# Smaller token blocks early, and scores and outputs in one stretch, in a retention and bilinear FFN kernel

## The chip, the cores and the metric

The kernel runs on one core of one Trainium2 chip. The metric is the device time of one execution in microseconds (us), the median of several runs. Most executions of one kernel agree within 0.3%.

Engine names: PE is TensorE (matmul), PEld its weight loads, DVE is VectorE, ACT is ScalarE, POOL is GpSimd, SP is SyncE, whose queue (SPq) issues the DMAs.

## The reference, cut to what matters

```python
# q, k, v: [8 batches, 8 heads, 576 positions, 64]; weights 512 x 1536 (twice), 1536 x 512
scores = scale * q @ k.T
ret    = (scores * Dmat) @ v            # Dmat[i, j] = gamma_head ** (i - j) for i >= j, else 0
x      = ret.transpose(0, 2, 1, 3).reshape(4608, 512)
out    = ((x @ w_a) * (x @ w_b)) @ w_out
```

The kernel computes the first part in chunks of 128 tokens (36 chunks) with a running state, and the FFN in blocks of tokens. A block of n tokens needs n/128 finished chunks.

## The kernel before: the parts that matter

The FFN block is a generator. Each `yield` gives the cost of a matmul in units of a 512-column matmul, and says whether attention work may be put in at this place. `todo` holds attention work with its place, counted in those units.

```python
ps_ffn = pool("ps_ffn", 3, PS)      # three PSUM banks for pa, pb, po
ps_att = pool("ps_att", 4, PS)      # four for scores, outputs, transposes
...
def ffn_block(tok0, n, runs):
    for count in runs:
        for F in ...:               # 12 F steps: pa = xT . wa (4 matmuls of n columns)
            ...                     # ACT: ha = copy of pa
        for F in ...:               # pb = xT . wb (4 matmuls)
            ...
            nc.vector.tensor_tensor(hT[:, F, 0:n], has[F][:, 0:n], pb[:, 0:n], op=ALU.mult)
            pop()                   # one pending DVE piece: a mask multiply or a scaling
            yield n / 512, True
    for u in range(n // 128):       # po = hT . wo, 12 matmuls of 512 columns, copied out by ACT or DVE
        ...

def second_stage(g):                # states, then scores; the masks go to the pending list
    for i in g[1:]:
        state(i)
    for i in g:
        scores(i)

def third_stage(g):
    flush()                         # empties the pending list
    for i in g:
        outputs(i)                  # into an attention bank; the scaling goes to the pending list
...
blocks = [512, 256, 384, 384] + [512] * ((NTOK - 1536) // 512)
placed = [((6, 7), 145, 178, 194), ((8,), 166, 197, 207),     # chunks, cast, scores, outputs
          ((9, 10), 186, 224, 254)]                           # later pairs: scores 36 before outputs
...
for tb, n in enumerate(blocks):
    for cost, edge in ffn_block(tok, n, runs):
        at += cost
        while todo and edge and at >= todo[0][0]:
            _, fn, args = todo.pop(0)
            fn(*args)
    flush()                         # end of a block: everything pending is emitted at once
    tok += n
```

From chunk 6 on, q and k of a chunk are transposed by a DMA (`turn`), issued on the same SP queue as the loads of q, k, v and the stores of the result.

## Time and profile before

| | before |
|---|---|
| timed median | 346.02 us (345.85 to 346.22) |
| span of the profiled execution | 877.8 us |
| PE busy in it | 854.0 us (97%) |
| 512-column matmuls, start to start, in its timeline (most of them) | 0.62 us |

The profiled execution ran its matmuls 2.9 times slower than the timed ones. Lines of its page: span; busy time, share and instructions of PE and DVE; the chain that ended last.

```profile
span 877.8 us, 6134 instructions
PE 854.0 (97%) x2390; PEld 309.4 (35%) x2426; DVE 162.0 (18%) x272; ACT 112.6 (13%) x229; POOL 84.3 (10%) x121
...
PE 97%; issue 2%; DMA 1%; SPq 0%; POOL 0%; DVE 0%; ACT 0%
```

Groups of instructions of the same trace, by shape (busy us, mean ns of one, idle before and what ended it):

```profile
L349 PE MATMUL po<-wo_sb,hT 128*128 128x512 bf16 x401 | 246.1, 826 | 6.2 <-issue 6.2
...
L358 ACT COPY osb<-po 128x512 f32<-128x512 f32 x19 | 11.1, 586 | 212.7 <-PE po L349 201.8 <-remote 10.9
```

DMA queue timeline of the same trace (start, time the queue spent, instruction). The first line holds the loads back until the weights are in, the last two are transposes of chunks 6 and 7 (one merged line) and of chunk 10:

```profile
37.03 0.64 SPq L406 DMA_DIRECT2D gate<-wo_sb  x1
...
123.42 2.76 SPq L206 DMA_TRANSPOSE qkT<-qkb  x2
...
137.58 2.36 SPq L206 DMA_TRANSPOSE qkT<-qkb  x1
```

How to read it: PE is busy everywhere, and the little that is not PE is spread thin. But a PE at a third of its speed hides every wait for DMA or DVE that a full-speed PE would meet.

### The profile page before, as it was taken

Reading aid. Unit: us, or ns where it says so; the run is one execution under the profiler, and the core shown is the slowest. Engines: PE = TensorE matmul, PEld = TensorE weight load, DVE = VectorE, ACT = ScalarE, POOL = GpSimd, SP = SyncE. Lnnn points to the kernel's source line nnn. Section 1 sums busy time; section 2 is a strip of 40 time slices with the busy share of each in tenths; the row PEclk is TensorE's granted clock in tenths of the full one; section 3 lists DMA queues with packets and bytes.
Section 4 is the critical chain, followed back from the end, with each engine's and each line's share of the span. In section 5 each row is a group of like instructions: output and inputs, shape, how many; then the busy total and the mean of one; then the engine's idle time right before and its main releaser. Section 6 shows DMA issues by size and latency. Waiting matters only on the chain.

```text
span 877.8 us, 6134 instructions
## 1 busy us (share of the span) xinstructions
PE 854.0 (97%) x2390; PEld 309.4 (35%) x2426; DVE 162.0 (18%) x272; ACT 112.6 (13%) x229; POOL 84.3 (10%) x121
## 2 busy tenths in 40 slices
PE   6999999999999999999999999999999999999998
PEld 3322345344344333333333333432333333232223
DVE  4211122222121111211122112121121112201100
ACT  5111112011011101100111011101110011101110
POOL 6040002201011010002100210011000000000000
DMA  9980049350090041025400650066002300000000
GB/s 181 207 152 0 25 90 187 80 88 1 29 199 0 13 102 18 0 50 108 81 1 1 131 108 1 0 112 129 0 1 60 61 0 1 8 28 12 0 13 36
DMA packets 154333, 50.74 MB, mean 58 GB/s; under 512 B 144960, under 2 KB 149824, under 8 KB 154304
## 3 DMA queue, kind: packets, MB, share of 16 engines
q1 hardware_dynamic: 149552, 45.63, 26.6%
q0 software_dynamic: 4752, 4.72, 3.4%
q8 instruction: 19, 0.31, 0.2%
q14 instruction: 10, 0.08, 0.0%
HBM read 37.75 MB, written 9.44 MB: 54 GB/s over the span
## 4 chain that ended last, share of the span: by engine, by line
PE 97%; issue 2%; DMA 1%; SPq 0%; POOL 0%; DVE 0%; ACT 0%
PE pb L329 29%; PE pa L316 29%; PE po L349 28%; PE o L285 2%; PE kv L235 2%; PE o L277 2%; PE w L372 1%; PE tp L218 1%; DMA kf<-in_k_dram 1%; SPq L104 0%; POOL qkb L195 0%; PE sc_2460 L252 0%; PE sc_2449 L252 0%; PE sc_1402 L252 0%; PE sc_3677 L252 0%
## 5 line engine op out<-in xcount | busy, mean ns | idle before, releaser
L329 PE MATMUL pb<-xT,wb_sb 128*128 128x512 bf16 (+2 forms) x471 | 279.9, 775 | 2.7 <-issue 2.7
L316 PE MATMUL pa<-xT,wa_sb 128*128 128x512 bf16 (+2 forms) x472 | 277.3, 769 | 3.6 <-issue 3.1
L349 PE MATMUL po<-wo_sb,hT 128*128 128x512 bf16 (+1 forms) x425 | 253.2, 810 | 6.2 <-issue 6.2
L334 DVE TENSOR_TENSOR hT<-ha,pb 128x512 bf16<-128x512 bf16 (+2 forms) x120 | 76.2, 635 | 457.4 <-PE pb L329 443.3
L329 PEld LDWEIGHTS <-wb_sb 128*128 128x128 bf16 x480 | 82.8, 172 | 173.7 <-issue 168.0
L316 PEld LDWEIGHTS <-wa_sb 128*128 128x128 bf16 x480 | 80.7, 172 | 157.2 <-issue 151.4
L349 PEld LDWEIGHTS <-hT 128*128 128x128 bf16 x444 | 73.1, 169 | 162.1 <-issue 159.0
L322 ACT CAST ha<-pa 128x512 bf16<-128x512 f32 (+2 forms) x120 | 65.2, 544 | 447.1 <-PE pa L316 440.9
L196 POOL TENSOR_TENSOR vb<-vf,vs 128x512 bf16<-128x512 f32 x36 | 37.6, 1044 | 295.1 <-issue 144.3
L189 POOL CAST qkb<-qf 128x512 bf16<-128x512 f32 x30 | 18.3, 611 | 290.5 <-DMA qf<-in_q_dram 274.6
L360 DVE COPY osb<-po 128x512 f32<-128x512 f32 (+1 forms) x17 | 11.5, 676 | 175.5 <-PE po L349 175.5
L358 ACT COPY osb<-po 128x512 f32<-128x512 f32 (+1 forms) x20 | 11.5, 576 | 219.3 <-PE po L349 208.4
L292 DVE TENSOR_TENSOR xT<-o,qs 128x512 bf16<-128x512 f32 (+1 forms) x37 | 24.8, 674 | 46.8 <-PE o L285 46.8
L285 PE MATMUL o<-sT,vb 128*64 128x128 bf16 x288 | 30.4, 379 | 0.0
L235 PE MATMUL kv<-vb,qkb 128*128 128x128 bf16 (+1 forms) x128 | 25.4, 373 | 1.4 <-issue 0.9
L235 PEld LDWEIGHTS <-qkb 128*128 128x128 bf16 (+1 forms) x128 | 17.6, 161 | 22.2 <-issue 20.9
L285 PEld LDWEIGHTS <-vb 128*64 128x64 bf16 x288 | 22.3, 181 | 2.5 <-issue 2.5
L195 POOL CAST qkb<-kf 128x512 bf16<-128x512 f32 x32 | 19.7, 616 | 13.6 <-DMA kf<-in_k_dram 13.5
L252 PEld LDWEIGHTS <-qkT 64*128 64x128 bf16 x288 | 15.4, 135 | 12.6 <-issue 9.8
L218 PE MATMUL tp<-identity,qkb 128*128 128x128 bf16 x48 | 8.1, 362 | 6.0 <-ACT qkb L191 5.3
L372 PE MATMUL w<-identity 128*128 128x512 bf16 x14 | 9.3, 790 | 0.0
L218 PEld LDWEIGHTS <-qkb 128*128 128x128 bf16 x48 | 5.2, 140 | 11.1 <-ACT qkb L191 5.7
(195 smaller groups left out, 194.7 us busy)
## 6 DMA issues: line engine op xcount, KB each, us to landing
out_dram<-osb SPq DMA_DIRECT2D x35, 256.0 KB, 2.2
qf<-in_q_dram SPq DMA_DIRECT2D x32, 256.0 KB, 3.6
kf<-in_k_dram SPq DMA_DIRECT2D x32, 256.0 KB, 4.2
vf<-in_v_dram SPq DMA_DIRECT2D x32, 256.0 KB, 4.7
wo_sb<-in_moe_w_out_dram POOLq DMA_DIRECT2D x3, 512.0 KB, 17.8
qf<-in_q_dram SPq DMA_DIRECT2D x8, 128.0 KB, 3.6
kf<-in_k_dram SPq DMA_DIRECT2D x8, 128.0 KB, 3.5
vf<-in_v_dram SPq DMA_DIRECT2D x8, 128.0 KB, 3.5
```

The source lines that it names most:

```text
L189: nc.gpsimd.tensor_copy(qb, qf)
L195: nc.gpsimd.tensor_copy(kb, kf)
L196: nc.gpsimd.tensor_tensor(vb.rearrange("p (h d) -> p h d", h=H), vf.rearrange("p (h d) -> p h d", h=H), vs[:, i % PER, :].unsqueeze(2).to_ ...
L218: nc.tensor.transpose(tp[:, p, :], natural_qk[w][:, p * 128:(p + 1) * 128], identity)
L235: nc.tensor.matmul(kv[:, p, :], kb[r, sl], vb[r, sl], start=(m in (0, MID) and p == 0), stop=True, skip_group_check=True)
L285: nc.tensor.matmul(o[64 * hi:64 * hi + 64, p, :], vb[:, e0:e0 + 64], sT[:, hi, p, :], start=(m == 0 and p == 0), stop=True, skip_group_che ...
L292: nc.vector.tensor_tensor(xT[:, c0:c1, i * 128:(i + 1) * 128], o[:, c0:c1], qs[:, c0:c1, s0:s0 + 128], op=ALU.mult)
L316: nc.tensor.matmul(pa[:, 0:n], wa_sb[:, c, fs], xT[:, c, tok0:tok0 + n], start=(c == 0), stop=(c == NC - 1))
L322: nc.scalar.copy(ha[:, 0:n], pa[:, 0:n])
L329: nc.tensor.matmul(pb[:, 0:n], wb_sb[:, c, fs], xT[:, c, tok0:tok0 + n], start=(c == 0), stop=(c == NC - 1))
L334: nc.vector.tensor_tensor(hT[:, F, 0:n], has[F][:, 0:n], pb[:, 0:n], op=ALU.mult)
L349: nc.tensor.matmul(po[:, 0:width], hT[:, F, u * 128:(u + 1) * 128], wo_sb[:, F, cols], start=(F == 0), stop=(F == NF - 1))
```

## The change

The intent: (1) blocks of 256 tokens for chunks 4 to 15, so that the FFN needs chunks two at a time and later; (2) from chunk 14, the scores of a pair and the outputs of the pair before it in one stretch, which saves changes of the PE's tiling mode (scores use row tiles, outputs column tiles, the FFN neither). Since the scores then hold all four attention banks, the outputs go to FFN banks. (3) A reordered start, and more buffers.

```diff
-    blocks = [512, 256, 384, 384] + [512] * ((NTOK - 1536) // 512)
+    blocks = [512] + [256] * 6 + [512] * ((NTOK - 2048) // 512)
...
-        o = ps_att.tile([128, HP, 128], FP32, tag="att", name="o")
+        o = (home or ps_att).tile([128, HP, 128], FP32,
+                                  tag="ab" if home else "att", name="o")
...
+    def both_stages(g, following):
+        flush()
+        for i in following:
+            scores(i)
+        masks, later[:] = later[:], []
+        for i in g:
+            outputs(i, home=ps_ffn)
+            flush()
+        later.extend(masks)
...
-    placed = [((6, 7), 145, 178, 194), ((8,), 166, 197, 207),
-              ((9, 10), 186, 224, 254)]
+    placed = [((6, 7), 145, 176, 200), ((8, 9), 186, 238, 264),
+              ((10, 11), 222, 296, 324), ((12, 13), 280, 352, 384)]
...   # start, in the pass that ends with chunk 2: one mask, three of four weight issues,
...   # the casts of chunk 3, then the other mask; the fourth weight issue comes later
```

More of the change, by code (lines that the diff above doesn't have):

```diff
@@ L72 @@
     stage = pool("stage", 5)
-    nat = pool("nat", 5)
-    qkt_pool = pool("qkt", 6)
+    nat = pool("nat", 7)
+    qkt_pool = pool("qkt", 8)
     st_pool = pool("st", 4)
     h_pool = pool("hT", 2)
-    ha_pool = pool("ha", 6)
+    ha_pool = pool("ha", 7)
     o_pool = pool("osb", 4)
@@ L162, in load_w @@
     def load_w(f0, f1):
-        nc.gpsimd.dma_start(wa_sb[:, :, f0:f1], wa_r[:, :, f0:f1])
-        nc.gpsimd.dma_start(wb_sb[:, :, f0:f1], wb_r[:, :, f0:f1])
+        for w_sb, w_r in ((wa_sb, wa_r), (wb_sb, wb_r)):
+            nc.gpsimd.dma_start(w_sb[:, :, f0:f1], w_r[:, :, f0:f1])
+            yield
     def load_wo(i):
@@ L264, in scores, with outputs @@
         later.append(lambda: masked(1))
-    def outputs(i, halves=False):
+    def outputs(i, halves=False, home=None):
         m = i % PER
@@ L300, in outputs @@
             later.append(lambda: scaled(0, HP))
-    blocks = [512, 256, 384, 384] + [512] * ((NTOK - 1536) // 512)
-    WCOLS = [3, 4, 5]
+    blocks = [512] + [256] * 6 + [512] * ((NTOK - 2048) // 512)
+    WRUNS = [3, 4, 5]
     def ffn_block(tok0, n, runs):
@@ L374, in warm @@
                              start=True, stop=True)
-    W1, W2 = 128 * WCOLS[0], 128 * (WCOLS[0] + WCOLS[1])
+    W1, W2 = 128 * WRUNS[0], 128 * (WRUNS[0] + WRUNS[1])
     idle = {0: (0, 0), 1: (0, 3), 2: (2, 4), 3: (1, 4)}
@@ L387 @@
         scores(i)
-        flush()
+        pop()
         if i == 2:
-            load_w(0, W1)
-            load_w(W1, W2)
-        if i < 3:
-            cast(i + 1, "dve" if i == 2 else "act")
+            list(load_w(0, W1))
+            second = load_w(W1, W2)
+            next(second)
+        if i == 2:
+            cast(3, "dve")
+            flush()
+        else:
+            flush()
+            if i < 3:
+                cast(i + 1, "act")
         state(i)
@@ L400 @@
             flush()
-    load_w(W2, DFF)
+    list(second)
+    list(load_w(W2, DFF))
     for i in (0, 1, 2):
@@ L449, in third_stage, with sums @@
             outputs(i)
+    def both_stages(g, following):
+        flush()
+        for i in following:
[3 more added lines that the diff above has]
+            outputs(i, home=ps_ffn)
+            flush()
+        later.extend(masks)
+    def sums(g):
+        for i in g:
+            state(i)
     def one_by_one(what, i):
@@ L468 @@
                  for at, what in zip(places, "CTSA")]
-    placed = [((6, 7), 145, 178, 194), ((8,), 166, 197, 207),
-              ((9, 10), 186, 224, 254)]
-    limit = 1e9
-    for i in range(NCH - 1, 10, -2):
-        g = (i, i + 1) if i + 1 < NCH else (i,)
-        third = min(starts[i] - 16, limit - 60)
-        limit = third
-        placed.append((g, third - 104, third - (30 if i == 11 else 36), third))
+    placed = [((6, 7), 145, 176, 200), ((8, 9), 186, 238, 264),
+              ((10, 11), 222, 296, 324), ((12, 13), 280, 352, 384)]
     for g, zeroth, second, third in placed:
         todo += [(zeroth, ahead, (g[-1],)), (second - 14, first_stage, (g,)),
-                 (second, second_stage, (g,)), (third, third_stage, (g,))]
+                 (second, second_stage, (g,))]
+        if g != placed[-1][0]:
+            todo.append((third, third_stage, (g,)))
+    merged = []
+    limit = 1e9
+    for i in range(NCH - 2, 13, -2):
+        third = min(starts[i] - 16, limit - 58)
+        limit = third
+        merged.insert(0, ((i, i + 1), third))
+    for (g, third), (following, _) in zip([(placed[-1][0], placed[-1][3])] + merged,
+                                          merged + [((), 0)]):
+        todo.append((third, both_stages, (g, following)))
+    for g, third in merged:
+        todo += [(third - 136, ahead, (g[-1],)),
+                 (third - 28, sums, (g[0:1],)), (third - 14, sums, (g[1:],))]
     todo.sort(key=lambda e: e[0])
@@ L484 @@
     for tb, n in enumerate(blocks):
-        runs = WCOLS if tb == 0 else [1] * NF
+        runs = WRUNS if tb == 0 else [1] * NF
         for cost, edge in ffn_block(tok, n, runs):
```

## The prediction

> **What bounds the kernel now.** The profiled execution is not the timed one: its span is 877.8 us, the timed median 346.02 us. In the trace's timeline 512-column matmuls follow each other every 0.62 us. The Trainium skill ("TensorE: Matmul & The Clock Gate", Back-to-back issue gap) gives N/2.4 + 2.5 ns, 216 ns for N = 512; no profile line shows it, but only it fits the timed runs. So I take DVE, ACT, POOL and DMA from the trace, PE from that formula.
>
> Estimate of the timed run: FFN 663,552 columns and 1,392 matmuls, 280 us; attention of chunks 4 to 35 about 490 steps (pairs counted once) of some 60 ns, 30 us (timeline: pairs start 55 to 80 ns apart in bursts); start-up about 22.5 us (first pa at 29.6 us in the trace); tail 4 us. Sum 336.5. About 9.5 us remain: 64 changes of tiling mode (16 groups, four each) and early waits. PE is the bound (chain of waits: PE 97%); gain can only come from those 9.5 us and the start.
>
> **Early waits.** The DMA queue's timeline holds q/k/v loads until 37.0 us (weights first); the last of chunk 8 is issued at 55.8 us. From the transpose of chunk 6 (123.4 us) to that of chunk 10 (137.6 us, plus 4.0 us landing) it takes 18 us. Timed, that starts near 59 us and ends near 78 to 81; PE wants scores of chunk 10 near 77. Estimated wait 1 to 4 us.
>
> **What the change does.**
> 1. Blocks of 256 move those scores from place 224 to 296 (15 us later), in pairs from the start: the early wait goes, -1 to -4 us.
> 2. Merged stages: scores next to outputs, three mode changes per pair in place of four, and one group fewer: 64 to 49. The skill ("TensorEngine Tiling (Array Packing)", Key Properties) says that a mode switch drains TensorE; the slow trace cannot show the cost. Estimate 0.1 us each: -1.5 us.
> 3. Start: mask 0 before the key cast on DVE, one weight issue (0.77 us on POOL) later: -0.5 us.
> 4. 192 more FFN matmuls: +0.5 us (2.5 ns each), up to +1.5 if weight loads show.
> 5. In 256-token blocks an F step is 0.87 us; DVE needs 0.42 (hT) + 0.69 (mask), so it lags after each pair's scores: +0.5 to 1.5 us.
> 6. Outputs take two of three FFN banks. In five places (16 units before a block) a po accumulation is open; if banks rotate strictly, the next po waits for the eviction of the one just finished (ACT copy 0.586 us plus signalling, about 0.8 us): +0 to +4 us. In pa/pb places the hT multiply (0.69 us) hides under the attention.
> More buffers, earlier casts: off the path.
>
> Sum: about -2 us.
>
> **Predicted 344.0 us**, range 340.0 to 348.0. Chances: faster by over 2% 0.06, within 2% 0.91, slower 0.03.
>
> **What would show it.** Right on 6: in the waits view po waits for ACT osb about five times, under 1 us each. Right on 5: pa waits for DVE hT in the small blocks. A profile again slow on PE hides the worth of 1 and 2.
>
> **What would make it wrong.** A mode change costing 0.2 us or more or a longer early wait (faster, 338 to 340); weight loads exposed in every 256-column matmul, or DVE lag chaining through the banks (slower, 349 and more).

## The result, and the profile after

The kernel after takes 346.54 us (346.25 to 346.68, 4 runs), the kernel before 345.94 us on the same chip (345.74 to 346.22, 4 runs). The ratio is 1.0016, 95% interval 0.9999 to 1.0033: no gain, and if anything 0.6 us lost. (A ratio is the mean time of one kernel's fast runs over that of the other's of the same rounds, so it is not quite the ratio of the medians.) The range held the time, but the forecast gain of 2 us did not come.

This trace ran at full PE speed. Its page:

```profile
span 345.0 us, 6595 instructions
PE 328.9 (95%) x2587; PEld 190.3 (55%) x2618; DVE 163.3 (47%) x297; ACT 115.5 (33%) x252; POOL 84.9 (25%) x121
...
PEclk9999999999999999999999999999999999999999
DMA  9999999999799999749399139933994230020002
```

For a fair comparison the kernel before was run once more (run before_again), and that trace was fast too:

> The kernel before, unchanged, for a trace at full TensorE speed (the one given ran its matmuls 2.9 times slower). Time 346 us. If the account of the prediction holds: a first pa near 21.4 us (0.7 later than after's 20.69), mode changes of 93 to 99 ns as in the trace of after, some 64 of them, and a wait of 1 to 4 us before the scores of chunk 10. Rival: the early wait is not there (under 0.5 us) and the two kernels tie because the change removed nothing but a few mode changes.

It took 346.1 us (one run, state unknown; its span of 344.4 us is that of a fast run). Its page:

```profile
span 344.4 us, 6170 instructions
PE 330.4 (96%) x2426; PEld 171.5 (50%) x2426; DVE 160.8 (47%) x272; ACT 112.3 (33%) x229; POOL 85.0 (25%) x121
...
PEclk9999999999999999999999999999999999999999
DMA  9999999999999994911994099507990950020002
```

The DMA row says that the DMA engines are full for the first third of the span in both kernels.

With two traces at full speed a ledger can be made. For each matmul I take the time to the start of the next one, less N/2.4 + 2.5 ns. That is the spacing that the Trainium skill gives for an isolated matmul ("TensorE: Matmul & The Clock Gate", Back-to-back issue gap; for streams it gives less, see the last section). The traces agree with it: the 12 pb matmuls from 23.27 to 25.86 us in the trace of after are 215.8 ns apart. What is left over is a gap, and gaps that equal a matmul missing from the trace are set aside. (In the small blocks none is missing; there every gap over 30 ns counts.) From the first pa to the end:

| ledger, us | before_again | after | after less before |
|---|---|---|---|
| first pa of the FFN | 21.33 | 20.69 | -0.64 |
| 192 more matmuls at 2.5 ns | | | +0.48 |
| changes of tiling mode (76 and 61 in the traces) | 7.28 | 5.84 | -1.44 |
| waits before scores or between outputs up to chunk 12 | 3.10 | 2.40 | -0.70 |
| gaps inside 256-token blocks, between pa, pb | 0.16 | 3.24 | +3.08 |
| sum | | | +0.8 |

The spans differ by 0.6 us. So the two kernels do not tie because nothing happened: 2.8 us were won and 3.6 us lost. Three of these rows need their lines.

**Mode changes.** Timeline of PE, before_again: outputs at 185.92 us, and scores by themselves at 192.57 us:

```profile
184.96 1.03 PE L329 MATMUL pb<-xT,wb_sb 128*128 128x512 bf16 x4
185.92 0.41 PE L277 MATMUL o<-qkT,state 128*64 128x128 bf16 x8
...
192.57 0.62 PE L252 MATMUL sc<-qkT 64*128 64x128 bf16 x16
193.12 1.25 PE L349 MATMUL po<-wo_sb,hT 128*128 128x512 bf16 x5
```

The same in after: scores and outputs in one stretch:

```profile
185.23 1.03 PE L331 MATMUL pb<-xT,wb_sb 128*128 128x512 bf16 x4
186.19 0.62 PE L253 MATMUL sc<-qkT 64*128 64x128 bf16 x16
186.74 0.41 PE L279 MATMUL o<-qkT,state 128*64 128x128 bf16 x8
...
187.75 1.04 PE L318 MATMUL pa<-xT,wa_sb 128*128 128x512 bf16 x3
```

In both, four pb matmuls take 0.863 us and the next start comes 0.96 us after the first: the change of mode costs 95 ns, here and at nearly every other place (92 to 99 ns in these two traces). The expectations below count 57 and 68 changes in program order where the traces show 61 and 72; the difference is the same.

**Early waits.** Timeline of before_again (the bracket is the idle time and what ended it): chunks 7, 10 and 12 wait for their transposes.

```profile
64.78 0.40 PE L252 MATMUL sc<-qkT 64*128 64x128 bf16 x8
65.36 0.40 PE L252 MATMUL sc<-qkT 64*128 64x128 bf16 x8 [0.18 <-DMA qkT<-qkb]
...
80.97 0.40 PE L252 MATMUL sc<-qkT 64*128 64x128 bf16 x8 [1.30 <-DMA qkT<-qkb]
...
93.03 0.40 PE L252 MATMUL sc<-qkT 64*128 64x128 bf16 x8 [0.78 <-DMA qkT<-qkb]
```

In after, chunks 10 and 12 do not wait any more, but chunks 6 and 7 do. The first line is the DMA queue, which issues their transposes:

```profile
60.10 3.35 SPq L207 DMA_TRANSPOSE qkT<-qkb  x2
...
62.86 0.39 PE L236 MATMUL kv<-vb,qkb 128*128 128x128 bf16 x4
...
64.60 0.40 PE L253 MATMUL sc<-qkT 64*128 64x128 bf16 x8 [1.36 <-DMA qkT<-qkb]
...
65.82 0.40 PE L253 MATMUL sc<-qkT 64*128 64x128 bf16 x8 [0.82 <-DMA qkT<-qkb]
```

Chunk 7 starts at 65.36 us in one kernel and at 65.82 us in the other. PE arrives 1.6 us earlier in after and waits for nearly the same moment. (A bracket counts from the modelled end of a matmul; the ledger counts from start to start and so gives 1.42 and 0.98 us.)

**Small blocks.** Timeline of after around the start of a 256-token block, DVE and PE:

```profile
112.97 0.69 DVE L362 COPY osb<-po 128x512 f32<-128x512 f32 x1 [1.41 <-PE po L351]
...
113.58 1.88 DVE L259 TENSOR_TENSOR sT<-sc,mask 128x512 bf16<-128x512 f32 x3
...
115.37 0.74 DVE L336 TENSOR_TENSOR hT<-ha,pb 128x256 bf16<-128x256 bf16 x2
...
115.83 0.60 PE L331 MATMUL pb<-xT,wb_sb 128*128 128x256 bf16 x4 [0.46 <-ACT ha L324]
```

The `flush()` at the end of a block puts three mask multiplies on DVE in a row. The first hT of the new block stands behind them, so the pb banks of the first two F steps stay taken. As I read the lines, one bank is then left to take turns: the pa of the third step uses it, and its pb starts only when the ACT copy of that pa is done. So the wait names ACT, and the cause is DVE. Three banks of 256 columns hold 3 x 0.44 = 1.3 us of PE work, less than the 1.88 us of the masks.

### The profile page after: what moved, and what is told of

Its sections match the earlier page's. It is cut to its first block, busy times and chain, and to the rows that moved or that the text cites. A ratio compares the mean times of both kernels' runs of the same rounds, so it can differ in the third digit from the quotient of the medians.

```text
span 345.0 us, 6595 instructions
## 1 busy us (share of the span) xinstructions
PE 328.9 (95%) x2587; PEld 190.3 (55%) x2618; DVE 163.3 (47%) x297; ACT 115.5 (33%) x252; POOL 84.9 (25%) x121
## 4 chain that ended last, share of the span: by engine, by line
PE 79%; DMA 11%; SPq 5%; POOL 2%; issue 1%; ACT 0%; POOLq 0%
PE po L351 24%; PE pa L318 24%; PE pb L331 23%; SPq L104 5%; DMA wo_sb<-in_moe_w_out_dram 4%; DMA vf<-in_v_dram 3%; PE sc L253 2%; PE o L279 2%; PE o L287 2%; PE kv L236 2%; DMA qf<-in_q_dram 1%; DMA kf<-in_k_dram 1%; DMA qkT<-qkb 1%; POOL vb L197 1%; POOL wa_sb L164 1%
## 5 line engine op out<-in xcount | busy, mean ns | idle before, releaser
L336 DVE TENSOR_TENSOR hT<-ha,pb 128x512 bf16<-128x512 bf16 (+1 forms) x144 | 79.4, 553 | 95.8 <-PE pb L331 91.5
L331 PE MATMUL pb<-xT,wb_sb 128*128 128x512 bf16 (+1 forms) x573 | 115.5, 325 | 1.2 <-ACT ha L324 0.9
L318 PE MATMUL pa<-xT,wa_sb 128*128 128x256 bf16 (+1 forms) x567 | 114.9, 325 | 1.0 <-DVE xT L294 0.5
L324 ACT CAST ha<-pa 128x512 bf16<-128x512 f32 (+1 forms) x144 | 69.0, 479 | 137.8 <-PE pa L318 131.5
L351 PE MATMUL po<-wo_sb,hT 128*128 128x512 bf16 (+1 forms) x425 | 97.1, 373 | 1.4 <-issue 0.6
L331 PEld LDWEIGHTS <-wb_sb 128*128 128x128 bf16 x576 | 56.3, 98 | 38.8 <-issue 1.3
L318 PEld LDWEIGHTS <-wa_sb 128*128 128x128 bf16 x576 | 54.8, 98 | 38.2 <-issue 1.7
L351 PEld LDWEIGHTS <-hT 128*128 128x128 bf16 x444 | 42.0, 98 | 44.9 <-issue 0.2
L259 DVE TENSOR_TENSOR sT<-sc,mask 128x512 bf16<-128x512 f32 x72 | 47.3, 683 | 6.0 <-PE sc L253 5.3
L287 PE MATMUL o<-sT,vb 128*64 128x128 bf16 x288 | 14.1, 222 | 0.0
```

What stands on the lines that cost most here:

```text
L259: nc.vector.tensor_tensor(sT[:, hi], ps[hi], keep.unsqueeze(1).to_broadcast([128, HP, 128]), op=ALU.mult)
L287: nc.tensor.matmul(o[64 * hi:64 * hi + 64, p, :], vb[:, e0:e0 + 64], sT[:, hi, p, :], start=(m == 0 and p == 0), stop=True, skip_group_che ...
L318: nc.tensor.matmul(pa[:, 0:n], wa_sb[:, c, fs], xT[:, c, tok0:tok0 + n], start=(c == 0), stop=(c == NC - 1))
L324: nc.scalar.copy(ha[:, 0:n], pa[:, 0:n])
L331: nc.tensor.matmul(pb[:, 0:n], wb_sb[:, c, fs], xT[:, c, tok0:tok0 + n], start=(c == 0), stop=(c == NC - 1))
L351: nc.tensor.matmul(po[:, 0:width], hT[:, F, u * 128:(u + 1) * 128], wo_sb[:, F, cols], start=(F == 0), stop=(F == NF - 1))
```

## The experiments

All of these are correct against the reference. Each is given with its ratio to the kernel before in the same rounds (after itself: 1.0016). Names that begin with a are edits of after, those with b of before.

| run | median us | ratio, 95% interval |
|---|---|---|
| a_spread | 346.16 | 1.0002 (0.9989 to 1.0015) |
| a_spread_late | 345.04 | 0.9971 (0.9958 to 0.9984) |
| b_blocks | 347.99 | 1.0066 (1.0047 to 1.0085) |
| b_start | 346.13 | 1.0000 (0.9984 to 1.0016) |
| a_noflush | 345.53 | 0.9983 (0.9963 to 1.0003) |
| a_spread2_late | 343.11 | 0.9901 (0.9889 to 0.9914) |
| a_unmerged | 349.34 | 1.0093 (1.0071 to 1.0115) |
| b_later | 346.12 | 0.9994 (0.9978 to 1.0009) |
| a_load8 | 350.33 | 1.0118 (1.0100 to 1.0136) |
| a_spread2_late_load8 | 348.36 | 1.0058 (1.0041 to 1.0076) |
| a_spread2_late_unmerged | 350.42 | 1.0118 (1.0104 to 1.0132) |
| a_best_again | 343.08 | 0.9907 (0.9892 to 0.9922) |
| a_best_unmerged60 | 344.11 | 0.9939 (0.9926 to 0.9951) |

My theory after the ledger: the small blocks lose through DVE bursts, the early wait is PE coming too early for transposes that the DMA queue times, and the mode changes are worth what they count. The rival to the first: a 256-column step is itself slow, in whatever order. The rival to the second: later chunks wait instead. The rival to the third: the merge gives back what it saves.

### a_spread and a_noflush: the bursts

```diff
# a_spread
-                pop()
+                if n > 256 or F % 2:
+                    pop()
                 yield n / 512, True
...
# a_spread and a_noflush: end of a block
-        flush()
         tok += n
```

> The kernel after, with the pending mask multiplies spread: in 256-token blocks one goes after every second F step, and the emptying of the list at the end of a block is dropped, so they no longer run three or four in a row on DVE ahead of the hT multiplies. Theory A (the small blocks lose 3.1 us because those bursts hold FFN banks): waits inside small blocks fall from 3.1 us to under 1 us in the trace, time 343.5 to 344.5 us. Rival B (a 256-column matmul is itself slower, or its eviction is, and the bursts only show where the loss surfaces): waits move but their sum stays, time 346 to 347 us.

The gaps in small blocks fell from 3.24 to 1.25 us, nearly as far as theory A said, but the time fell by only 0.4 us: outputs of chunks 8 to 11 now waited 1.88 us for their own masks, which I had thinned too much. Waits had moved, which is half of what rival B said. So only one part was undone:

> The kernel after, with one thing taken out: the emptying of the pending list at the end of each block (a_spread also thinned the masks, which made outputs of chunks 8 to 11 wait 1.9 us for masks and blurred the verdict). Theory A (the two bursts of three and four masks at the ends of blocks cost some 0.9 and 1.1 us of the 3.1): small-block waits fall to about 1.5 us and no outputs wait, time 1.0 to 1.8 us under after. Rival B (DVE work per F step is what counts, in whatever order): waits stay near 3 us, time within 0.4 us of after.

Ratio 0.9983 against 1.0016 for after: about 1.1 us gained by removing one line, and gaps of 2.19 us in place of 3.24. The intervals of the two ratios overlap a little, so the time alone would not settle it; the gaps agree with it. (In this trace the first pa came 0.84 us later than in that of after, and the wait for chunks 6 and 7 was 1.1 us shorter; the two nearly cancel.) The masks now alternate with hT on DVE:

```profile
113.60 0.68 DVE L259 TENSOR_TENSOR sT<-sc,mask 128x512 bf16<-128x512 f32 x1
114.20 0.41 DVE L336 TENSOR_TENSOR hT<-ha,pb 128x256 bf16<-128x256 bf16 x1
114.53 0.69 DVE L259 TENSOR_TENSOR sT<-sc,mask 128x512 bf16<-128x512 f32 x1
```

The gaps came out 0.7 us above the 1.5 expected, but the time is inside what theory A expected and outside rival B. The rest of the gaps is steady lag: a mask and an hT together take about 1.1 us on DVE by their lengths, and one such pair follows the other after 0.93 us here, against 0.87 us of PE work in one F step.

### b_blocks: the small blocks in the kernel before

```diff
-    blocks = [512, 256, 384, 384] + [512] * ((NTOK - 1536) // 512)
+    blocks = [512] + [256] * 6 + [512] * ((NTOK - 2048) // 512)
```

> The kernel before with only the block sizes of after (places of chunks 11 and up follow from them). Theory A: 192 more matmuls +0.5 us, bank waits in small blocks +2 to +3 us, the wait for chunk 12 (0.95 us) goes: 347.5 to 348.5 us. Rival B (small blocks as such help because they want chunks later): at or under 346 us.

347.99 us, as theory A expected, but not wholly for its reason. Its trace (one of its two slower executions, 349.5 us) has 3.16 us of gaps in small blocks, and 1.5 us of these are no bank waits. They follow the wait for chunk 10, when TensorE was granted about half its clock. Below are that wait and a line of windows (stretch, its length, busy time of each engine with instructions, granted PE clock, DMA share, GB/s), where the clock is 0.55:

```profile
81.07 0.47 PE L252 MATMUL sc<-qkT 64*128 64x128 bf16 x8 [2.14 <-DMA qkT<-qkb]
...
81.50:85.00 3.50, 3.50 (x21) 2.55 (x20) 1.02 (x2) 0.74 (x2) 1.37 (x3) 0.55 1.25 264
```

The four faster executions (347.6 to 348.1 us) list a mean clock of 1.00, the two slower ones 0.994 and 0.995. That leaves 1.6 us of bank waits, less than the 2 to 3 us expected. The wait for chunk 12 is gone and that for chunk 10 is 2.30 us, longer than before's 1.46. Small blocks with the places of before are a loss of about 2 us here, a part of it in the wait for chunk 10.

### b_start and b_later: what is won early is waited away

```diff
# b_start: the start of after alone, in the kernel before
-        flush()
+        pop()
         if i == 2:
-            load_w(0, W1)
-            load_w(W1, W2)
+            list(load_w(0, W1))        # load_w now yields between its two issues
+            second = load_w(W1, W2)
+            next(second)
+            cast(3, "dve")
+            flush()
...
# b_later: b_start, and scores of 9, 10 and of 11, 12 one F step later
-              ((9, 10), 186, 224, 254)]
+              ((9, 10), 186, 232, 254)]
-        placed.append((g, third - 104, third - (30 if i == 11 else 36), third))
+        placed.append((g, third - 104, third - (24 if i == 11 else 36), third))
```

> The kernel before with only the start of after (mask, key cast, one weight issue). Theory A: the first pa comes 0.6 us earlier, but the wait for the transpose of chunk 7, whose time the DMA queues set, grows by the same: time within 0.3 us of before, that wait 0.35 to about 1 us in the trace. Rival B: the start is worth its 0.6 us: 345.3 us.

The first pa came at 20.60 us, 0.73 earlier, and the time did not change (ratio 1.0000). The lines of the trace show where it went:

```profile
64.50 0.40 PE L253 MATMUL sc<-qkT 64*128 64x128 bf16 x8 [0.26 <-DMA qkT<-qkb]
65.38 0.40 PE L253 MATMUL sc<-qkT 64*128 64x128 bf16 x8 [0.48 <-DMA qkT<-qkb]
```

Chunk 7 starts at 65.38 us, against 65.36 us in the kernel before. By start-to-start gaps the wait for chunks 6 and 7 grew from 0.35 to 0.96 us. One caution: the traces of kernels with the new start have their first pa between 20.60 and 21.53 us, those of the two with the old start at 21.33 and 21.43. So what the start is worth has a scatter as large as itself. The timed runs say that none of it arrives, to within their interval of about 0.55 us.

> b_start with the scores of chunks 9, 10 one F step later (place 232 for 224) and of 11, 12 one step later (24 for 30 before their outputs). Theory A (these waits of 1.46 and 0.95 us are TensorE coming too early for transposes whose time the DMA queues set): both waits nearly go, time 1.6 to 2.3 us under b_start, near 344.2 us. Rival B (the transposes come as much later, or the wait shows up at the next chunks): within 0.4 us of b_start.

This was a miss. The waits of chunks 10 and 12 did vanish from its trace, but the time stayed at that of b_start. Two things took their place in the profiled execution: outputs of chunk 10 waited 0.86 us for a mask (my later place left too little room), and chunks 6 and 7 waited 2.4 us, for transposes that came up to 1.4 us later than in b_start. They were issued only 0.28 us later (60.30 against 60.02 us), so most of the delay came after the issue. My edit does not touch what comes before them. Whether that lateness is chance or usual in this version I did not settle; rival B fits the time.

### a_spread_late and a_spread2_late: PE comes later, masks are thinned only where there is room

```diff
# both, against a_spread
-    placed = [((6, 7), 145, 176, 200), ...
+    placed = [((6, 7), 145, 184, 200), ...
# a_spread2_late
-                if n > 256 or F % 2:
+                if n > 256 or F % 2 or tok0 < 1280:
                     pop()
```

> a_spread, and the scores of chunks 6 and 7 at place 184 in place of 176. Theory A (the transposes of 6 and 7 land at a time set by the DMA queues, near 64.6 and 65.8 us; TensorE merely comes too early by 2.4 us): the wait before them falls to about 1 us, time 1.3 us under a_spread. Rival B: what comes later then waits instead (outputs of 7 for the masks, or the next transposes), time within 0.4 us of a_spread.

345.04 against 346.16 us in the same rounds: 1.1 us, from moving the scores of chunks 6 and 7 by two F steps. In its trace the two follow each other without a wait (one merged line of 16, where after has two of 8 with a wait before each):

```profile
64.89 0.62 PE L253 MATMUL sc<-qkT 64*128 64x128 bf16 x16
```

Outputs of chunk 7 wait 0.54 us for a mask, so a part was given back.

> As a_spread_late, but masks are thinned to every second F step only from chunk 10 on, where outputs come late enough. Theory A: the 1.9 us that outputs of chunks 8 to 11 waited in a_spread goes, small-block waits about 1 us, time 343.0 to 343.6 us. Rival B: 344.5 to 345.5 us, as a_spread_late.

343.11 us, inside what theory A expected, and the best of all: 1% under before, and 1.1% under after (0.9901 over 1.0016). Gaps in small blocks are 1.51 us, the wait for chunk 7 is 0.72 us, and no output waits. Against after that is 1.7 us and 1.7 us less, 3.4 us by the ledger for the 3.4 us between the medians (taken on two chips). The two losses named by the ledger are thus real, and together they are what hid the gain.

### a_load8 and a_spread2_late_load8: who sets the time of the transposes

```diff
-    for i in range(4, 9):
+    for i in range(4, 8):
         load(i)
...
-    counts = {"cast": 4, "load": 9}
+    counts = {"cast": 4, "load": 8}
```

> The kernel after with the loads of q, k, v of chunk 8 issued after the transpose of chunk 7 in place of before the transposes of 6 and 7 (the DMA queue works in order: in the trace of after the transpose of 6 has its inputs cast at 56.4 us and is issued at 60.1, behind the loads of chunk 8 and four output stores). Theory A (queue order sets the early wait): transposes of 6 and 7 land 1 to 3 us earlier, the wait before their scores (2.4 us) falls under 1 us, time 1 to 2 us under after. Rival B (the DMA engines are full up to there, so the loads of chunk 7 come no earlier and its transpose neither): wait within 0.6 us of 2.4, time within 0.5 us of after.

The mechanism of theory A is right. The transposes were issued at 57.69 instead of 60.10 us, and the wait of 2.4 us is gone entirely. The first line is the DMA queue:

```profile
57.69 2.74 SPq L207 DMA_TRANSPOSE qkT<-qkb  x2
...
64.04 0.62 PE L253 MATMUL sc<-qkT 64*128 64x128 bf16 x16
```

So the early wait is set by the order in the queue: the transposes stood behind the loads of chunk 8. But the time is worse than that of after, by 3.5 us (1.0118 against 1.0016). Every later load now came one chunk later, and chunk 15 pays:

```profile
117.42 0.40 PE L253 MATMUL sc<-qkT 64*128 64x128 bf16 x8
...
121.39 0.44 PE L253 MATMUL sc<-qkT 64*128 64x128 bf16 x8 [3.57 <-DMA qkT<-qkb]
```

And the wait is paid twice. Windows of this trace (stretch, its length, busy time of each engine with instructions, granted PE clock, DMA share, GB/s):

```profile
122.00:125.00 3.00, 3.00 (x40) 2.39 (x37) 1.33 (x2) 0.37 (x1) 1.09 (x2) 0.50 1.19 266
```

After 3.6 us of idleness the granted clock is 0.50 for the next three microseconds. The skill says as much: in "TensorE: Matmul & The Clock Gate", What's actually happening, the clock falls to half after at least one idle window of about 3.4 us. This trace agrees. That of b_blocks does not: there an idle time of 2.14 us was followed by a clock of 0.55. The measurement decides, so a wait shorter than the page's window can cost the clock too.

> The best version so far (343.1 us) with the same move of the loads of chunk 8. Theory A: the last 0.7 us of waiting for chunk 7 goes, 342.3 to 342.8 us. Rival B: within 0.3 us of 343.1, or slower because chunk 8 itself comes late (a new wait near place 238).

348.36 us, slower by 5.3 us than a_spread2_late: the new wait of 4.1 us at chunk 15 and a slow clock after it, a miss for theory A in time. Rival B named a late chunk; it was a later one than I had said.

### The merge undone: a_unmerged, a_spread2_late_unmerged, a_best_unmerged60

```diff
-        todo.append((third, both_stages, (g, following)))
+        todo.append((third, third_stage, (g,)))           # outputs in attention banks
+        if following:                                     # _ is the place of their outputs
+            todo.append((_ - 36, just_scores, (following,)))
# a_spread2_late_unmerged: _ - 40; a_best_unmerged60: _ - 36, outputs 60 places apart, not 58
```

> The kernel after with the merge undone: from chunk 14 scores stand alone 36 places before their outputs, and outputs go back to the attention banks; 68 changes of tiling mode after the first pa in place of 57. Theory A (each change costs 95 ns): 1.0 us slower than after, 347.4 to 347.8 us. Rival B (the merge is worth nothing, or its use of FFN banks costs what it saves): within 0.4 us of after.

349.34 us, 2.8 us slower than after, far more than expected. The trace has 1.05 us more in mode changes, but also four waits of 0.77 us of outputs for masks: with the places rounded to the ends of F steps, the last mask went out just ahead of the outputs. Together that is more than 2.8 us, and the gaps in small blocks were 1.6 us less than in after (1.67 for 3.24). The verdict is blurred.

> The best version so far with the merge undone, scores 40 places before their outputs so that their masks are done (in a_unmerged they were not, and outputs waited 3.2 us for masks, which blurred it); 68 mode changes in place of 57. Theory A (95 ns each): 1.0 us slower than a_spread2_late, near 344.1 us. Rival B (the merge is worth nothing): within 0.3 us of it.

350.42 us. Mode changes cost 1.02 us more, and no output waited, but second scores waited 1.23 us in each of four places and 0.96 us in a fifth, 5.9 us in all, for attention banks that outputs still held. A second miss.

> a_spread2_late once more, as the partner on the same chip of the run below. Theory: 343.1 us again, 0.99 of before. Rival: its gain was a matter of that chip, 345 us or more.

343.08 us, ratio 0.9907: the best version repeats.

> The same with the merge undone, this time with the spacing that the kernel before uses (outputs 60 places apart, scores 36 ahead of them), so that neither masks nor attention banks should be waited for (both spoiled the first two tries). Theory A (11 more mode changes at 95 ns and nothing else): 0.8 to 1.4 us slower than a_best_again. Rival B (merging is worth nothing): within 0.3 us. Rival C (apart, the two stages cannot be placed free of waits: outputs or scores wait again): 2 us or more slower, with waits between o or between sc matmuls in the trace.

344.11 us against 343.08 on the same chip: 1.03 us by the medians, 1.1 us by the ratios. Its trace has no large waits, and about 1.0 us more in mode changes. Theory A holds in time: 11 changes of about 95 ns. The two traced executions differ by less (343.84 and 343.21 us), since a_best_again waited 0.63 us for chunk 7 in its trace and this version did not; so the traces alone do not show that nothing else changed. Rival C was true of the two tries before, where the places were badly chosen.

## Why the prediction was wrong

It forecast 344.0 us, 2 us faster. The time was 346.54 us, within the range, but 0.6 us slower where a gain was forecast. Point by point, in the prediction's numbering:

1. **Failed: "the early wait goes, -1 to -4 us".** The wait at chunk 10 was there (1.46 us) and did go, and so did that at chunk 12. But after calls for the scores of chunks 6 and 7 at place 176 (before: 178), with a start 0.6 us earlier, and their transposes come at a time set by the order of the DMA queue. The wait came back there, 2.40 us in place of 3.10 in all: -0.7 us. I had looked at the chunk where before waits, and not asked where after would.
2. **Right.** 15 changes fewer. The number of each was twelve off (76 and 61 in the traces, against 64 and 49), because I had left out chunks 4 and 5 and the state matmuls of 64 rows (64*128 in the trace), which switch the mode too. 95 ns each, against an estimate of 0.1 us, is -1.4 us. a_best_unmerged60 shows it in time for 11 of the 15.
3. **Right in the trace, worth nothing in time.** The first pa came 0.64 us earlier in this pair of traces (with the scatter named at b_start); b_start shows that the next wait for a transpose takes it back (in the ledger of after, the loss is in the row of the early waits). It should not have been counted, since the prediction itself held that such a wait follows.
4. **Right by calculation.** 192 matmuls at 2.5 ns; no run measured this term alone, but 256-column matmuls keep to the formula where nothing waits.
5. **Failed in size: "+0.5 to 1.5 us".** It was +3.1 us. I costed one mask per F step. I overlooked that the `flush()` at the end of a block sends up to four masks at once, just where the next small block needs DVE. a_noflush gives 1.1 us for that alone.
6. **The condition was false, so +0.** The banks do not rotate strictly: in the instruction list of after, at the five places the next po waits for DVE, not for the ACT copy of the po just finished. I read that as the bank of an output. The waits view has no po waiting for osb.

Terms 1 and 5 were off by 1.8 and 2.1 us from the middle of what I gave (-2.5 and +1). Term 6, with about +1 us in the sum, was too high and hid part of this: -2 + 1.8 + 2.1 - 1 is +0.9 us, near the +0.6 measured.

## What to carry to other kernels

A shorter block shortens the time for which a fixed number of banks hides a burst on the evicting engine. Before halving a block, look for places where deferred work is emitted all at once, and spread it. In a stretch that a DMA queue times, work saved ahead of the wait is worth nothing until other PE work is moved in front of the wait; here eight places were worth 1.1 us, more than the whole reordered start. And when a profile was taken with the main engine slow, take a full-speed trace before trusting any statement about waits.

## What the Trainium skill lacked or had wrong

- "TensorEngine Tiling (Array Packing)", Key Properties, says that changing the tiling mode drains TensorE, but not what it costs. In the full-speed traces here it costs 91 to 100 ns per change at full clock, in any direction, where nothing else is waited for.
- "TensorE: Matmul & The Clock Gate", Back-to-back issue gap, gives sustained spacings with weight loads of about 131 ns for N = 512 and 81 ns for N = 128, and calls N/2.4 + 2.5 an isolated gap. Here the long streams with one weight load per matmul keep to N/2.4 + 2.5: 215.8 ns for N = 512.
- The same page's clock states (What's actually happening and Seeing it yourself: full, half, 13/16, and a quarter in which it has been seen stuck) have none that fits the first profile: most 512-column matmuls start 0.62 us apart, which is 0.82 GHz, all through the execution of 878 us, while the record lists a granted clock of 1.00. No run here shows why.
- The same page's idle window of about 3.4 us (What's actually happening) is no safe limit: in b_blocks 2.14 us of idle time were followed by a clock of 0.55.
- No page that I drew on says what an ordered DMA queue costs a transpose: here transposes came out 2.4 us later for standing behind the loads of one chunk (60.10 against 57.69 us).
